# A layernorm, spectral filter and GELU block: reordered table and filter loads, and accumulating transfers released by other waits

## The chip, the cores and the metric

The kernel runs on one core of a Trainium2 chip. The time of a run is the device time in microseconds (us) of one execution. The kernel before was timed in three runs. One more execution was profiled, and every duration below comes from it.

The engines are called as in the profile: PE is TensorE (matrix multiplies, with PEld its weight loads), DVE is VectorE, ACT is ScalarE, POOL is GpSimd and SP is SyncE. SP does no arithmetic here; it issues most of the transfers, one after the other, in a fixed order.

## The reference

```python
xn = layernorm(x)                                   # x: 2048 rows of 640, bf16
A  = irfft2(rfft2(xn) * (w_r + 1j * w_i))           # filter of 2048 x 321 complex numbers
B  = gelu(xn @ w1 + b1) @ w2 + b2                   # w1: 640 x 1536, w2: 1536 x 640
out = x + A + B
```

All inputs and the output are bf16. The two Fourier transforms are two-dimensional, over the 2048 rows and the 640 columns.

## The kernel before

**Tiles.** The 2048 rows are 16 tiles of 128 (tile c holds the rows c, c+16, ...). A tile is normalized on DVE (`stats`, `mv`, and the subtraction and scaling at L709), with the power of -1/2 on POOL (L683). Normalized tiles lie in one of three buffers for two tiles each, two of which are inside `T` and one is `U`.

**The dense branch.** The normalized tile is turned into `xnT` (columns on the partitions): tiles 0 to 3 by PE (L727), tiles 4 to 15 by a transposing transfer that SP issues (L718). The first product, in blocks of 4, 2, 2, 4 and 4 tiles, reads `xnT` and the first weight matrix (both weight matrices are called `W` in the profile); a block's PE instruction has 512 columns for four tiles and 256 for two. GELU (L802, ACT) makes `gT`. The second product reads `gT` and the second matrix, whose four loads are called w2, w2#1, w2#2 and w2#3; each row of 640 outputs is a pair of PE instructions with 512 and 128 columns.

**The spectral branch.** DVE folds a normalized tile with its mirror image (L742, L746), PE multiplies it with the table `gtab` (first step along the rows, result `XV`), then with `etab` (columns; result `Xb`), then with small blocks of `mtab` (result `Y`). DVE multiplies `Y` with the filter `Wf` (L907, result `T`; eight pairs of row groups, two such products a pair: k = 0 with the real part, k = 1 with the imaginary part) and adds (L911, `Z`). The way back is `ntab` (result `U`, in three buffers, two of which lie in the old space of `gtab` and `T`), a transposing transfer of `U` into `XV` (L933, sixteen of them, v0 to v15), `getab`, and `htab`, which adds the branch to the output in PE's accumulators. For all matmuls PE's line is the helper's, L553, and for copies out of the accumulators the lines are L564 (ACT) and L565 (DVE).

**The filter's loads.** `Wf` is read by 26 transfers of SP (L548). W0 is the real part, W1 the imaginary part: #0 to #3 are direct pieces (16 runs of 10 KB), #4 to #8 are mirrored pieces in runs of 642 bytes (#4, #5, #6 of 80 KB, #7 of 10 KB, #8 of 70 KB). Wl0 and Wl1 with #0 to #3 are the mirrored pieces (80 KB each) for the second half of the pairs. A filter product waits for all nine pieces of its part:

```python
filt_ops.append(K.op([("dve", dve_us(4 * KP, 2))], pr, lambda e, _, k=k, Y=Y, TB=TB, pair=pair: e.tensor_tensor(
    ...
    reads=[Y, B_wpad] + (B_w + B_wl if pair == 7 else [B_w[k]] if pair < 3 else [B_w[k], B_wl[k]]), writes=[TB], after=ring_ops))
```

**The accumulating transfers.** x + b2 is made in 32 bit, tile by tile: ACT writes b2 into a buffer (L995), and a transfer issued by POOL adds the tile of x to it (L1013; xo0 to xo15, 128 rows of 2560 bytes written). The buffers are old space of `X` (eight tiles) and of `xnT` (eight tiles: 13, 14, 0, 4, 6, 9, 12, 15). DVE adds this to the dense branch's result (L1019, for ten tiles called kept) or to the final sum (L1028). In the kernel before, each of these sixteen transfers waits for every W0 and W1 piece to land and for the last transposes of `xnT`; those of tiles 6, 9, 12 and 15 also wait for v0 to v15.

**What sets the order.** Each engine runs its own list in order. The list comes from a planner inside the kernel, which picks among the ready steps by a rank (one number a step in the table `RANK`), with the table `LAND` of how long each transfer takes from issue to landing. SP's order is written by hand in `SPQ`:

```python
line = [key[k + "#0" if "#" not in k else k] for k in SPQ]
for a, b in zip(line, line[1:]):
    b.gate.append(a)
```

A `gate` fixes only the order, `deps` make a semaphore wait.

Of the kernel before, what the change touches and what calls it, by code (L numbers as in the profile page):

```python
# [194 lines left out]
LAG = 1.6  # L195


LAND = {"x0#0": 2.38, "x1#0": 2.35, "w1_0_0#0": 3.37, "b1t#0": 2.88, "w1_0_1#0": 3.83, "x2#0": 3.78, "w1_0_2#0": 3.84, "w1_0_3#0": 3.87, "x3#0": 4.21, "w1_0_4#0": 4.72, "w1_1_0#0": 5.66, "w1_1_2#0": 6.24, "w1_1_4#0": 6.12, "x4#0": 5.84, "g#0": 7.46, "x6#0": 7.79, "x8#0": 7.97, "x10#0": 8.16, "x12#0": 8.72, "x14#0": 3.56, "b2#0": 3.37, "W0#0": 3.66, "W0#1": 3.95, "W0#2": 5.89, "W0#3": 5.88, "W1#0": 6.17, "W1#1": 6.16, "W1#2": 6.45, "W1#3": 6.44, "e#0": 6.13, "m#0": 5.89, "n#0": 5.6, "w2#0": 3.39, "w2#1": 4.28, "w2#2": 5.16, "w2#3": 6.05, "W0#4": 6.54, "W0#5": 6.46, "W0#6": 6.38, "W0#7": 5.81, "W0#8": 5.66, "W1#4": 5.58, "W1#5": 5.5, "W1#6": 5.42, "W1#7": 4.85, "W1#8": 4.7, "i#0": 3.97, "h#0": 4.79, "xnT8#0": 3.2, "xnT9#0": 3.2, "xnT10#0": 6.58, "xnT11#0": 6.43, "xnT12#0": 6.86, "xnT13#0": 6.71, "xnT14#0": 7.14, "xnT15#0": 6.99, "v0#0": 2.9, "v1#0": 2.9, "v2#0": 2.9, "v3#0": 2.9, "v4#0": 2.9, "v5#0": 2.9, "v6#0": 2.9, "v7#0": 2.9, "v8#0": 2.9, "v9#0": 2.9, "v10#0": 2.9, "v11#0": 2.9, "v12#0": 2.9, "v13#0": 2.9, "v14#0": 2.9, "v15#0": 2.9, "xo0#0": 13.37, "out#0": 2.92, "xo1#0": 6.0, "out#1": 1.9, "xo2#0": 6.0, "out#2": 1.9, "xo3#0": 6.27, "out#3": 1.9, "xo4#0": 14.06, "out#4": 2.74, "xo5#0": 7.1, "out#5": 2.53, "xo6#0": 6.0, "out#6": 1.9, "xo7#0": 7.93, "out#7": 2.2, "xo8#0": 8.65, "out#8": 1.9, "xo9#0": 6.0, "out#9": 1.9, "xo10#0": 10.46, "out#10": 1.9, "xo11#0": 11.16, "out#11": 1.9, "xo12#0": 6.12, "out#12": 2.63, "xo13#0": 11.89, "out#13": 1.9, "xo14#0": 12.66, "out#14": 2.33, "xo15#0": 7.14, "out#15": 1.9, "out#16": 1.9, "out#17": 1.9, "xnT4#0": 4.05, "xnT5#0": 3.66, "xnT6#0": 3.2, "xnT7#0": 3.2, "Wl0#0": 4.62, "Wl0#1": 4.54, "Wl0#2": 4.46, "Wl0#3": 4.38, "Wl1#0": 4.3, "Wl1#1": 4.22, "Wl1#2": 4.14, "Wl1#3": 4.06}

LAT = {"pe": 0.2, "dve": 0.125, "act": 0.16, "pool": 0.12}  # L200

# [873 lines left out]
```

## Time and profile before

| | |
|---|---|
| runs of the kernel before | 148.05, 149.12, 149.16 us (median 149.12) |
| profiled execution, its own time | 149.41 us |
| its span, first to last instruction | 147.6 us |
| granted TensorE clock | 1.000 |
| PE busy | 142.5 us, 1734 matmuls |
| DVE busy | 116.1 us |
| ACT busy | 78.4 us |
| POOL busy | 23.7 us |
| packets of SP's queue, as a share of 16 DMA engines | 54.8% |
| packets of POOL's queue | 15.4% |

Rows of the page and of the queries name the engine, the source line and the tiles as out<-in; "x4" counts instructions, and a bracket at a row's end is the idle time before it and what ended it. Time in rows runs from the first instruction. About 1.8 us of the execution's own time lie around the span.

### The profile page before, as it was taken

The numbers are of one execution on the slowest core, as the hardware profiler recorded it, in microseconds if no ns is written. First come the engines' busy times: TensorE is split into PE (matmuls) and PEld (weight loads), VectorE is DVE, ScalarE is ACT, GpSimd is POOL, SyncE is SP. The second block draws the span as 40 slices with busy tenths as digits, with TensorE's granted clock in tenths as the row PEclk, the third lists the DMA queues.
The fourth block names the chain that finished last, engine by engine and source line by source line (L and its number), as shares of the span: only waits on it lengthen the run. The fifth ranks groups of instructions, "written<-read, shape, count | busy, mean of one in ns | idle before, by whom it ended". The sixth has DMA issues, their size and how long they took to land.

```text
span 147.6 us, 4154 instructions
## 1 busy us (share of the span) xinstructions
PE 142.5 (97%) x1734; PEld 88.5 (60%) x1734; DVE 116.1 (79%) x242; ACT 78.4 (53%) x136; POOL 23.7 (16%) x54
## 2 busy tenths in 40 slices
PE   7999999999899999999999989999999999999993
PEld 7898558988456454445464444455556666565573
DVE  2989999999895236989754977597625999899993
ACT  3113997999969876885643554870303620402300
POOL 4321112312000003995000000000002600000000
DMA  4999899699936634999999909206353891231324
GB/s 124 278 322 408 221 152 203 105 378 307 147 68 162 139 92 102 207 272 318 274 276 98 128 0 128 54 5 123 62 112 66 172 229 47 88 120 63 133 89 133
DMA packets 31810, 23.64 MB, mean 160 GB/s; under 512 B 20656, under 2 KB 28592, under 8 KB 31664
## 3 DMA queue, kind: packets, MB, share of 16 engines
q1 hardware_dynamic: 29456, 18.14, 54.8%
q0 software_dynamic: 2336, 5.25, 15.4%
q8 instruction: 13, 0.21, 0.6%
q14 instruction: 5, 0.04, 0.2%
HBM read 13.54 MB, written 2.62 MB: 110 GB/s over the span
## 4 chain that ended last, share of the span: by engine, by line
PE 67%; DMA 11%; DVE 10%; SPq 8%; issue 1%
PE ps L553 67%; SPq L548 7%; DMA X<-in_A_x_dram 6%; DMA xnT<-T 5%; DVE stats L678 4%; DVE T L907 2%; SPq L718 1%; DVE mv L681 1%; DVE T L746 1%; DVE T L742 1%; DVE Y L565 1%; DVE T L565 1%; DVE U L709 0%; DVE T L709 0%; DVE W L1028 0%
## 5 line engine op out<-in xcount | busy, mean ns | idle before, releaser
L553 PE MATMUL ps<-xnT,W 128*128 128x512 bf16 (+2 forms) x384 | 57.3, 301 | 1.0 <-DMA xnT<-T 0.9
L553 PE MATMUL ps<-W,gT 128*128 128x512 bf16 (+3 forms) x396 | 57.1, 295 | 0.0
L553 PEld LDWEIGHTS ps<-W,gT 128*128 128x128 bf16 x396 | 30.0, 98 | 23.0 <-issue 1.5
L553 PEld LDWEIGHTS ps<-xnT,W 128*128 128x128 bf16 x384 | 31.5, 98 | 19.5 <-issue 2.2
L802 ACT ACTIVATE gT<-ps,b1col 128x512 bf16<-128x512 f32 (+1 forms) x60 | 33.7, 619 | 3.8 <-PE ps L553 3.6
L1013 POOL DMA_DIRECT2D xnT<-in_A_x_dram x8 | 9.9, 2778 | 44.9 <-DMA XV<-T 44.9
L678 DVE BATCH_NORM_STATS2 stats<-X 128x6 f32<-128x320 bf16 x32 | 14.0, 476 | 2.5 <-DMA X<-in_A_x_dram 2.4
L564 ACT ACTIVATE Wf<-ps 128x960 bf16<-128x960 f32 (+1 forms) x8 | 6.7, 866 | 16.6 <-PE ps L553 16.6
L907 DVE TENSOR_TENSOR T<-Y,Wf 128x1288 bf16<-128x1288 bf16 x16 | 12.5, 824 | 0.1
L565 DVE CAST Xb<-ps 128x960 bf16<-128x960 f32 (+1 forms) x6 | 6.7, 1119 | 6.3 <-PE ps L553 6.3
L683 POOL TENSOR_TENSOR rstd<-mv,mhalf 128x2 f32<-128x2 f32 (+1 forms) x10 | 7.1, 710 | 25.0 <-DVE mv L681 25.0
L565 DVE CAST Y<-ps 128x644 bf16<-128x644 f32 x8 | 6.5, 826 | 5.4 <-PE ps L553 5.4
L564 ACT ACTIVATE Xb<-ps 128x960 bf16<-128x960 f32 (+1 forms) x6 | 6.8, 1142 | 6.4 <-PE ps L553 6.4
L1019 DVE TENSOR_TENSOR X<-ps,X 128x640 f32<-128x640 f32 x8 | 6.6, 821 | 4.4 <-PE ps L553 4.4
L746 DVE TENSOR_TENSOR T<-T 128x128 bf16<-128x128 bf16 (+1 forms) x32 | 9.0, 315 | 0.1
L1013 POOL DMA_DIRECT2D X<-in_A_x_dram x8 | 7.2, 2068 | 9.4 <-DMA Wf<-in_A_w_i_dram 9.4
L564 ACT ACTIVATE Y<-ps 128x644 bf16<-128x644 f32 x8 | 5.6, 711 | 4.4 <-PE ps L553 4.4
L911 DVE TENSOR_TENSOR Z<-T 128x644 bf16<-128x644 bf16 x16 | 7.0, 488 | 1.0 <-PE ps L553 1.0
L967 DVE TENSOR_TENSOR Wf<-Wf 128x960 bf16<-128x960 bf16 (+1 forms) x12 | 6.8, 598 | 0.6 <-ACT Wf L564 0.4
L564 ACT ACTIVATE XV<-ps 128x512 bf16<-128x512 f32 (+4 forms) x10 | 7.1, 744 | 0.4 <-PE ps L553 0.3
L553 PE MATMUL ps<-etab,XV 32*128 32x160 bf16 (+1 forms) x128 | 7.2, 232 | 0.0
L1028 DVE TENSOR_TENSOR W<-ps,xnT 128x640 bf16<-128x640 f32 (+2 forms) x10 | 6.7, 686 | 0.6 <-PE ps L553 0.6
(61 smaller groups left out, 140.6 us busy)
## 6 DMA issues: line engine op xcount, KB each, us to landing
X<-in_A_x_dram POOLq DMA_DIRECT2D x8, 320.0 KB, 10.3
xnT<-in_A_x_dram POOLq DMA_DIRECT2D x8, 320.0 KB, 10.8
out_dram<-W SPq DMA_DIRECT2D x15, 160.0 KB, 1.8
X<-in_A_x_dram SPq DMA_DIRECT2D x6, 320.0 KB, 8.5
W<-in_B_w_dram SPq DMA_DIRECT2D x4, 480.0 KB, 5.1
W<-in_B_w_dram SPq DMA_DIRECT2D x6, 192.0 KB, 4.1
W<-in_B_w_dram SPq DMA_DIRECT2D x2, 384.0 KB, 5.6
Wf<-in_A_w_r_dram SPq DMA_DIRECT2D x4, 160.5 KB, 5.6
```

What stands on the lines that cost most here:

```text
L548: return K.op([(q, 0.7 if q == "pool" else issue)], prio, lambda e, _: e.dma_start(dst, src), writes=[buf], after=after, rows=rows, gate=g ...
L553: ins = e.matmul(o_, lhsT=lw, rhs=rh, start=st, stop=sp_, skip_group_check=True)
L564: return e.activation(dst(), src(), ACT.Copy, scale=scale)
L565: return e.tensor_copy(dst(), src())
L678: o = K.op([("dve", 0.393)], pr, lambda e, _, c=c, h=h: e.bn_stats(stats[:, c, 6 * h:6 * h + 6], view(X, c * D + H2 * h, [[1, H2]])), read ...
L683: K.op([("pool", 0.65)], 500, lambda e, _, a=a, b=b: e.tensor_tensor(out=rstd[:, a:b], in0=mv[:, a:b, 1], in1=mhalf[:, a:b], op=ALU.pow), ...
L746: ring_ops.append(K.op([("dve", dve_us(4 * w, 2))], pr, lambda e, _, op=op, x1v=x1v, xfv=xfv, o_=o_, o0=o0, o1=o1, w=w: e.tensor_tensor(ou ...
L802: g_op = K.op([("act", act_us(128 * nt, 1))], pr + PRIO["gelu"] + GP[bi], lambda e, _, c0=c0, nt=nt, fc=fc, hps=hps: e.activation(gT[:, fc ...
L907: filt_ops.append(K.op([("dve", dve_us(4 * KP, 2))], pr, lambda e, _, k=k, Y=Y, TB=TB, pair=pair: e.tensor_tensor(out=view(TT, TB.slot * 8 ...
L911: K.op([("dve", dve_us(2 * KP, 2))], pr, lambda e, _, TB=TB, Z=Z, r=r, op=op: e.tensor_tensor(out=view(Zb, Z.slot * 4 * KP + r * KP, [[2 * ...
L967: K.op([("dve", dve_us(320 * n, 2))], pr + 2, lambda e, _, k=k, op=op, yo=yo, y2=y2, n=n: e.tensor_tensor(out=view(Wf, Y2 + y2.slot * 3 * ...
L1013: xo_ops[c] = K.op([("pool", 0.9)], 51 - c / 20, lambda e, _, c=c, xov=xov: e.dma_start(xov(0, D), xv[:, c, :], accum_op=ALU.add), reads=[ ...
```

## The change

The change has four edits.

1. `SPQ`: the four w2 loads move from behind the transposes of tile 9 in between the transposes of tiles 8 and 9 and behind them; the tables e (`etab`), m (`mtab`), n (`ntab`) and the piece W0#2 move from ahead of the transposes of tiles 10 and 11 to behind them, with more of the filter's pieces; the transposes v0 to v3 now stand ahead of the tables i (`getab`) and h (`htab`) in SP's list.
2. The accumulating transfers no longer wait for the filter's pieces, only for the transposes of `xnT`.
3. The accumulating transfers of tiles 0 and 4 now wait for v0 to v15 (`LATEXO`).
4. `RANK` and `LAND` are replaced throughout, so the planner orders every engine anew. The line numbers L460 to L1034 grow by one.

```diff
 RANK = """
-612 351 350 590 594 349 596 588 593 353 273 408 285 305 557 274 237 295 290 289 232 278 362 106 270 473 473 473 359 473 473 473 473 473 473 473 473 473 473 473 473 473
...
+207 636 638 328 442 633 499 402 528 524 381 384 376 364 383 345 388 389 399 471 377 380 529 659 342 542 542 542 443 542 542 542 542 542 542 542 542 542 542 542 542 542
...
-SPQ = ('x0 x1 w1_0_0 w1_0_1 x2 w1_0_2 w1_0_3 x3 w1_0_4 w1_1_0 x4 w1_1_2 w1_1_4 g x6 x8 x10 x12 xnT4 xnT5 x14 b2 W0 W0#1 xnT6 xnT7 xnT8 xnT9 w2 w2#1 w2#2 w2#3 e m n W0#2 '
-       'xnT10 xnT11 W0#3 W1 xnT12 xnT13 W1#1 W1#2 xnT14 xnT15 W1#3 W0#4 W0#5 W0#6 W0#7 W0#8 W1#4 W1#5 W1#6 W1#7 W1#8 Wl0 Wl0#1 Wl0#2 Wl0#3 Wl1 Wl1#1 Wl1#2 Wl1#3 i h').split()
+SPQ = ('x0 x1 w1_0_0 w1_0_1 x2 w1_0_2 w1_0_3 x3 w1_0_4 w1_1_0 x4 w1_1_2 w1_1_4 g x6 x8 x10 x12 xnT4 xnT5 x14 b2 W0 W0#1 xnT6 xnT7 w2 xnT8 w2#1 xnT9 w2#2 w2#3 '
+       'xnT10 xnT11 W0#2 W0#3 W1 W1#1 W1#2 e xnT12 xnT13 m n W1#3 W0#4 xnT14 xnT15 W0#5 W0#6 W0#7 W0#8 W1#4 W1#5 W1#6 W1#7 W1#8 Wl0 Wl0#1 Wl0#2 Wl0#3 Wl1 Wl1#1 Wl1#2 Wl1#3 v0 v1 v2 v3 i h v4').split()
...
+LATEXO = (0, 4)
...
         for c in range(16):
-            xo_ops[c].gate += [WL[-1], TD[15]]
-            xo_ops[c].deps += WL + list(TD.values())
+            xo_ops[c].deps += list(TD.values()) + (v_ops if c in LATEXO else [])
             xo_ops[c].deps += v_ops if c in HOME[4:] else []
```

`LAND` is one long line of numbers and is left out.

The new ranks move instructions on every engine. The first place is on DVE, where the first filter products stand. In brackets are the semaphores that a row waits for: d_46 to d_49 and d_61 to d_65 tell of the nine pieces of W0, d_50 to d_53 and d_66 to d_70 of the nine pieces of W1. Before:

```order
118 L565 CAST Xb<-ps 128x2x2x160 [waits s_pe]
119 L565 CAST Xb<-ps 128x3x2x160 [waits s_pe]
120 L565 CAST Y<-ps 128x2x322 [waits s_pe] x2
121 L907 TENSOR_TENSOR T<-Y,Wf 128x1288 [waits d_61,d_49,d_62,d_48,d_63,d_47,d_64,d_46,d_65,s_dve]
122 L907 TENSOR_TENSOR T<-Y,Wf 128x1288 [waits s_act]
123 L565 CAST Xb<-ps 128x3x2x160 [waits s_pe]
124 L907 TENSOR_TENSOR T<-Y,Wf 128x1288 [waits d_53,d_66,d_52,d_67,d_51,d_68,d_50,d_69,d_70]
125 L907 TENSOR_TENSOR T<-Y,Wf 128x1288
126 L911 TENSOR_TENSOR Z<-T 128x2x322 [waits s_dve]
```

And now (a line number is one higher than before):

```order
115 L566 CAST Xb<-ps 128x2x2x160 [waits s_pe]
116 L566 CAST Xb<-ps 128x3x2x160 [waits s_pe]
117 L566 CAST Y<-ps 128x2x322 [waits s_pe] x2
118 L908 TENSOR_TENSOR T<-Y,Wf 128x1288 [waits d_66,d_53,d_67,d_52,d_68,d_51,d_69,d_50,d_70,s_dve]
119 L908 TENSOR_TENSOR T<-Y,Wf 128x1288 [waits d_61,d_49,d_62,d_48,d_63,d_47,d_64,d_46,d_65,s_act]
120 L566 CAST Xb<-ps 128x3x2x160 [waits s_pe]
121 L1020 TENSOR_TENSOR X<-ps,X 128x640 [waits d_607]
122 L908 TENSOR_TENSOR T<-Y,Wf 128x1288 x2
123 L912 TENSOR_TENSOR Z<-T 128x2x322 [waits s_dve] x2
```

The first product to be run, once two `Xb` and two `Y` copies are done, waited for W0; it now waits for W1, whose last piece W1#8 is issued last of the eighteen. One `Xb` copy stands between the first two products and the next two in both.

The second place is on PE, from the end of the first second-product steps (pairs of 512 and 128 columns) to the first product with `etab`. Before, 8 + 7 + 10 + 8 instructions of the first product with 512 columns (`ps<-xnT,W`) stand there, and three groups with `gtab`:

```order
54 L553 MATMUL ps<-W,gT 128x512
55 L553 MATMUL ps<-W,gT 128x128
56 L553 MATMUL ps<-xnT,W 128x512 x8
57 L553 MATMUL ps<-gtab,T 128x64x2 x10
58 L553 MATMUL ps<-xnT,W 128x512 x7
59 L553 MATMUL ps<-gtab,T 128x64x2 x10
60 L553 MATMUL ps<-xnT,W 128x512 x10
61 L553 MATMUL ps<-gtab,T 128x64x2 x10
62 L553 MATMUL ps<-xnT,W 128x512 x8
63 L553 MATMUL ps<-etab,XV 128x160 x16
64 L553 MATMUL ps<-xnT,W 128x512 x5
65 L553 MATMUL ps<-etab,XV 128x160 x24
```

Now there are 2 + 8 + 7 of them at this place:

```order
54 L554 MATMUL ps<-W,gT 128x512
55 L554 MATMUL ps<-W,gT 128x128
56 L554 MATMUL ps<-xnT,W 128x512 x2
57 L554 MATMUL ps<-gtab,T 128x64x2 x10
58 L554 MATMUL ps<-xnT,W 128x512 x8
59 L554 MATMUL ps<-gtab,T 128x64x2 x10
60 L554 MATMUL ps<-xnT,W 128x512 x7
61 L554 MATMUL ps<-etab,XV 128x160 x16
62 L554 MATMUL ps<-xnT,W 128x512 x5
63 L554 MATMUL ps<-etab,XV 128x160 x24
```

Three more stand further up, between the first two blocks of second-product steps:

```order
40 L554 MATMUL ps<-W,gT 128x512
41 L554 MATMUL ps<-W,gT 128x128
42 L554 MATMUL ps<-xnT,W 128x512 x3
43 L554 MATMUL ps<-gtab,T 128x64x2 x10
44 L554 MATMUL ps<-W,gT 128x512
45 L554 MATMUL ps<-W,gT 128x128
```

So 20 instead of 33 of these 512-column instructions come ahead of the first `etab` group. One `gtab` group of ten (counted over the whole list) has moved from this stretch to a place ahead of the second product's first step; the groups ahead of `etab` are eight in both. Behind the first `etab` group both kernels run 5 instructions with 512 columns, 24 with `etab`, then 7 and 8 (now 8 and 7) with a group of `mtab` behind each.

More of the change, by code (lines that the diff above doesn't have):

```diff
@@ L195 @@
 LAG = 1.6
-LAND = {"x0#0": 2.38, "x1#0": 2.35, "w1_0_0#0": 3.37, "b1t#0": 2.88, "w1_0_1#0": 3.83, "x2#0": 3.78, "w1_0_2#0": 3.84, "w1_0_3#0": 3.87, "x3#0": 4.21, "w1_0_4#0": 4.72, "w1_1_0#0": 5.66, "w1_1_2#0": 6.24, "w1_1_4#0": 6.12, "x4#0": 5.84, "g#0": 7.46, "x6#0": 7.79, "x8#0": 7.97, "x10#0": 8.16, "x12#0": 8.72, "x14#0": 3.56, "b2#0": 3.37, "W0#0": 3.66, "W0#1": 3.95, "W0#2": 5.89, "W0#3": 5.88, "W1#0": 6.17, "W1#1": 6.16, "W1#2": 6.45, "W1#3": 6.44, "e#0": 6.13, "m#0": 5.89, "n#0": 5.6, "w2#0": 3.39, "w2#1": 4.28, "w2#2": 5.16, "w2#3": 6.05, "W0#4": 6.54, "W0#5": 6.46, "W0#6": 6.38, "W0#7": 5.81, "W0#8": 5.66, "W1#4": 5.58, "W1#5": 5.5, "W1#6": 5.42, "W1#7": 4.85, "W1#8": 4.7, "i#0": 3.97, "h#0": 4.79, "xnT8#0": 3.2, "xnT9#0": 3.2, "xnT10#0": 6.58, "xnT11#0": 6.43, "xnT12#0": 6.86, "xnT13#0": 6.71, "xnT14#0": 7.14, "xnT15#0": 6.99, "v0#0": 2.9, "v1#0": 2.9, "v2#0": 2.9, "v3#0": 2.9, "v4#0": 2.9, "v5#0": 2.9, "v6#0": 2.9, "v7#0": 2.9, "v8#0": 2.9, "v9#0": 2.9, "v10#0": 2.9, "v11#0": 2.9, "v12#0": 2.9, "v13#0": 2.9, "v14#0": 2.9, "v15#0": 2.9, "xo0#0": 13.37, "out#0": 2.92, "xo1#0": 6.0, "out#1": 1.9, "xo2#0": 6.0, "out#2": 1.9, "xo3#0": 6.27, "out#3": 1.9, "xo4#0": 14.06, "out#4": 2.74, "xo5#0": 7.1, "out#5": 2.53, "xo6#0": 6.0, "out#6": 1.9, "xo7#0": 7.93, "out#7": 2.2, "xo8#0": 8.65, "out#8": 1.9, "xo9#0": 6.0, "out#9": 1.9, "xo10#0": 10.46, "out#10": 1.9, "xo11#0": 11.16, "out#11": 1.9, "xo12#0": 6.12, "out#12": 2.63, "xo13#0": 11.89, "out#13": 1.9, "xo14#0": 12.66, "out#14": 2.33, "xo15#0": 7.14, "out#15": 1.9, "out#16": 1.9, "out#17": 1.9, "xnT4#0": 4.05, "xnT5#0": 3.66, "xnT6#0": 3.2, "xnT7#0": 3.2, "Wl0#0": 4.62, "Wl0#1": 4.54, "Wl0#2": 4.46, "Wl0#3": 4.38, "Wl1#0": 4.3, "Wl1#1": 4.22, "Wl1#2": 4.14, "Wl1#3": 4.06}
@@ new lines @@
+LAND = {"x0#0": 2.36, "x1#0": 2.39, "w1_0_0#0": 3.76, "b1t#0": 3.0, "w1_0_1#0": 3.74, "x2#0": 3.69, "w1_0_2#0": 4.21, "w1_0_3#0": 4.21, "x3#0": 4.21, "w1_0_4#0": 4.69, "w1_1_0#0": 5.25, "w1_1_2#0": 6.14, "w1_1_4#0": 7.73, "x4#0": 5.57, "g#0": 8.54, "x6#0": 8.68, "x8#0": 8.77, "x10#0": 9.05, "x12#0": 9.1, "x14#0": 4.49, "b2#0": 3.72, "W0#0": 4.5, "W0#1": 4.3, "W0#2": 6.0, "W0#3": 6.39, "W1#0": 6.78, "W1#1": 7.17, "W1#2": 7.56, "W1#3": 3.0, "e#0": 7.64, "m#0": 2.83, "n#0": 2.54, "w2#0": 3.55, "w2#1": 4.29, "w2#2": 5.02, "w2#3": 5.91, "W0#4": 3.18, "W0#5": 2.89, "W0#6": 2.89, "W0#7": 2.33, "W0#8": 2.71, "W1#4": 2.79, "W1#5": 2.8, "W1#6": 2.8, "W1#7": 2.24, "W1#8": 2.71, "i#0": 2.69, "h#0": 3.51, "xnT8#0": 4.24, "xnT9#0": 4.98, "xnT10#0": 6.6, "xnT11#0": 6.45, "xnT12#0": 4.06, "xnT13#0": 3.91, "xnT14#0": 3.69, "xnT15#0": 3.54, "v0#0": 2.9, "v1#0": 2.9, "v2#0": 2.9, "v3#0": 2.9, "v4#0": 2.9, "v5#0": 2.9, "v6#0": 2.9, "v7#0": 2.9, "v8#0": 2.9, "v9#0": 2.9, "v10#0": 2.9, "v11#0": 2.9, "v12#0": 2.9, "v13#0": 2.9, "v14#0": 2.9, "v15#0": 2.9, "xo0#0": 4.2, "out#0": 3.0, "xo1#0": 5.0, "out#1": 2.0, "xo2#0": 5.8, "out#2": 2.0, "xo3#0": 6.5, "out#3": 2.0, "xo4#0": 5.0, "out#4": 2.0, "xo5#0": 7.2, "out#5": 2.0, "xo6#0": 5.8, "out#6": 2.0, "xo7#0": 8, "out#7": 2.0, "xo8#0": 8.7, "out#8": 2.0, "xo9#0": 6.5, "out#9": 2.0, "xo10#0": 9.5, "out#10": 2.0, "xo11#0": 10.2, "out#11": 2.0, "xo12#0": 7.2, "out#12": 2.0, "xo13#0": 11, "out#13": 2.0, "xo14#0": 11.7, "out#14": 2.0, "xo15#0": 8, "out#15": 2.0, "out#16": 2.0, "out#17": 2.0, "xnT4#0": 5.07, "xnT5#0": 4.24, "xnT6#0": 4.03, "xnT7#0": 3.51, "Wl0#0": 2.79, "Wl0#1": 2.8, "Wl0#2": 2.8, "Wl0#3": 2.81, "Wl1#0": 2.81, "Wl1#1": 2.81, "Wl1#2": 2.82, "Wl1#3": 2.82}
```

34 rows, old and new, of the table RANK are left out of this document.

## The prediction

> **What bounds the kernel now.** I read the page first. Two of its rows matter:
>
> ```profile
> span 147.6 us, 4154 instructions
> PE 142.5 (97%) x1734; PEld 88.5 (60%) x1734; DVE 116.1 (79%) x242; ACT 78.4 (53%) x136; POOL 23.7 (16%) x54
> ```
>
> PE is idle for 5 of 147.6 us, so a change can win only what PE waits, and every new wait of PE counts in full. The waits of PE come next. Beside the one for the first instruction there are two:
>
> ```profile
> PE ps L553 <- DMA xnT<-T: 0.9, 1, 0.9
> PE ps L553 <- DVE T L907: 0.6, 1, 0.6
> ```
>
> PE's timeline says what they cost. Twelve second-product steps (six pairs) take 37.59 - 35.96 = 1.63 us, so the twelve from 38.15 should be followed at 39.78; PE goes on at 40.86, **1.08 us** late. Ahead of a group with small blocks the same twelve take 104.67 - 102.94 = 1.73, so the twelve from 83.67 should be followed at 85.40; PE goes on at 86.09, **0.69 us** late.
>
> ```profile
> 35.96 1.79 PE L553 MATMUL ps<-W,gT 128*128 128x512 bf16 x12
> 37.59 0.72 PE L553 MATMUL ps<-gtab,T 128*128 128x128 bf16 x10
> 38.15 1.79 PE L553 MATMUL ps<-W,gT 128*128 128x512 bf16 x12
> 40.86 1.89 PE L553 MATMUL ps<-xnT,W 128*128 128x512 bf16 x8 [0.92 <-DMA xnT<-T]
> 42.59 0.72 PE L553 MATMUL ps<-gtab,T 128*128 128x128 bf16 x10
> 49.66 0.97 PE L553 MATMUL ps<-etab,XV 128*128 128x160 bf16 x16
> ...
> 83.67 1.79 PE L553 MATMUL ps<-W,gT 128*128 128x512 bf16 x12
> 86.09 0.52 PE L553 MATMUL ps<-Z,ntab 32*32 32x320 bf16 x32 [0.62 <-DVE T L907]
> ...
> 102.94 1.80 PE L553 MATMUL ps<-W,gT 128*128 128x512 bf16 x12
> 104.67 0.51 PE L553 MATMUL ps<-Z,ntab 32*32 32x320 bf16 x32
> ```
>
> The first wait is for the transposes of tiles 10 and 11. They are issued at 31.81 and take 8.0 us, behind W2 (whose four loads take 5.1 in the median), three tables and W0#2:
>
> ```profile
> 31.81 2.73 SPq L718 DMA_TRANSPOSE xnT<-T  x2
> ...
> xnT<-T SPq DMA_TRANSPOSE x2, 8.0
> ...
> W<-in_B_w_dram SPq DMA_DIRECT2D x4, 480.0 KB, 5.1
> ```
>
> The second is named after DVE, but ACT's copy for the same group began at 85.18, after 1.60 us of waiting for a transpose of `U`, and so ended just ahead of PE's 86.09. The first two transposes of that kind took 8.8 us:
>
> ```profile
> 85.18 0.77 ACT L564 ACTIVATE U<-ps 128x512 bf16<-128x512 f32 x2 [1.60 <-DMA XV<-U]
> ...
> XV<-gtab SPq DMA_TRANSPOSE x2, 8.8
> ```
>
> These transposes share the DMA engines with the accumulating transfers, which POOL starts at 57.65, when W1's last piece has landed:
>
> ```profile
> 57.65 7.18 POOL L1013 DMA_DIRECT2D X<-in_A_x_dram  x8 [9.35 <-DMA Wf<-in_A_w_i_dram]
> ```
>
> **What the change removes.** Transposes 10 and 11 now stand behind the w2 loads alone, and those are issued some 2 us earlier. PE's first readers of them now stand right behind the first twelve second-product steps, and one group of `gtab` more (38.15 - 37.59 = 0.56) ahead of these: they are due at 37.59 + 0.56 = 38.15. The transposes are issued some 2 us earlier, near 30 and 31, and would need about 7 us to be late; the 8.0 had four more loads in it. I count this wait as gone: **-1.08**, with 0 as the other end. What is late next there is W2 for the steps now due at 35.96 + 0.56 = 36.5; its last load keeps its time, since two transposes stand among the earlier issues. For the second wait: the accumulating transfers start 10 us earlier (below), only nine of them run early, and `getab` and `htab` now stand behind v0 to v3, so the DMA engines are free for these: **-0.69**, or 0. The two tables' readers are PE's last stages, far behind. Both together are -1.77. The later place of e, m and n and of tiles 0 and 4 costs nothing as long as they land ahead of their readers, which are 3 us or more away; a table late by k us would cost k. The new order of equal work on DVE and ACT I bound by the smaller wait, -0.7 to +0.7, and take 0, since PE's queue covers it in all but two places now.
>
> **What it adds.** The filter's multiplication comes earlier. Up to the first `etab` group PE runs 13 fewer instructions of 512 columns. Eight of them take 42.59 - 40.86 = 1.73, so 13 are 2.81 us. With the wait gone, `etab` starts at 49.66 - 1.08 - 2.81 = 45.77, that is 3.89 earlier, and from there to the first filter product the work is the same. DVE's timeline has that product at 58.28:
>
> ```profile
> 38.77 1.22 DVE L565 CAST XV<-ps 128x1024 bf16<-128x1024 f32 x1
> 40.86 0.80 DVE L709 TENSOR_SCALAR T<-X,mv,rstd 128x640 bf16<-128x640 bf16 x2 [0.87 <-DMA xnT<-T]
> ...
> 58.28 1.57 DVE L907 TENSOR_TENSOR T<-Y,Wf 128x1288 bf16<-128x1288 bf16 x2
> 59.77 1.23 DVE L565 CAST Xb<-ps 128x960 bf16<-128x960 f32 x1
> 60.89 1.56 DVE L907 TENSOR_TENSOR T<-Y,Wf 128x1288 bf16<-128x1288 bf16 x2
> 65.41 1.57 DVE L907 TENSOR_TENSOR T<-Y,Wf 128x1288 bf16<-128x1288 bf16 x2
> ```
>
> So DVE is ready for it at 58.28 - 3.89 = **54.4**. Before, the first product read the real part W0; W1 was wanted only at 60.89. Now the first one reads W1, the last to land.
>
> When is W1#8 issued? SP first waits for the norm of tile 12. DVE starts it at 40.86, after 0.87 of waiting for the old transposes. That wait goes, and the reordered work ahead of it nets to some 1.9 us less (an estimate: two `XV` copies of 1.22 and shorter work go behind it, about half as much comes ahead). So it starts near 38.1 and ends, as one of two in 0.80, near 38.55. From there SP goes by its rows:
>
> ```profile
> 30.18 0.44 SPq L548 DMA_DIRECT2D mtab<-c_M  x1
> 41.33 2.54 SPq L718 DMA_TRANSPOSE xnT<-T  x2
> 45.18 2.60 SPq L718 DMA_TRANSPOSE xnT<-T  x2
> 48.46 3.86 SPq L548 DMA_DIRECT2D Wf<-in_A_w_r_dram  x5
> 52.36 3.16 SPq L548 DMA_DIRECT2D Wf<-in_A_w_i_dram  x5
> ...
> xnT<-T SPq DMA_TRANSPOSE x2, 2.9
> ```
>
> Two transposes take 2.58 (to the next issue), m and n twice 0.48, W1#3 and W0#4 twice 0.65: transpose 14 is issued at 43.4, 15 at 44.7, and it lands 2.9 later, at 47.6 to 47.7. **At 47.7 the accumulating transfers are let go.** SP goes on at 46.1: the five pieces W0#4 to #8 took 52.36 - 48.46 = 3.9, so #5 to #8 take 3.25; then W1#4 from 49.4, at 0.64 each, W1#8 at 52.0. So W0#8 (48.7) and all of W1#4 to #8 are issued after the accumulations began. The trace shows what that does to such loads, as KB and us to landing:
>
> ```profile
> Wf<-in_A_w_i_dram SPq DMA_DIRECT2D x3, 80.2 KB, 2.6
> Wf<-in_A_w_i_dram SPq DMA_DIRECT2D x1, 70.2 KB, 2.4
> ...
> Wf<-in_A_w_i_dram SPq DMA_DIRECT2D x1, 80.2 KB, 6.0
> ...
> Wf<-in_A_w_i_dram SPq DMA_DIRECT2D x1, 80.2 KB, 8.4
> ...
> X<-in_A_x_dram POOLq DMA_DIRECT2D x1, 320.0 KB, 6.1
> ...
> xnT<-in_A_x_dram POOLq DMA_DIRECT2D x4, 320.0 KB, 17.0
> ```
>
> Ahead of the accumulations an 80 KB piece lands after 2.6 us and W1#8 after 2.4. The four that SP issues right behind POOL's start at 57.65 take 6.0 (issued at 58.14, landed at 64.1) up to 8.4 (60.11, 68.5): the first lands 6.5 us after POOL's start, the others 1.46 apart. The accumulations land 6.1 after the first issue and, by the last row (17.0 from 62.9, nine to ten behind the first), about 1.7 apart.
>
> The contested pieces are now 70 + 3 x 80 + 10 + 70 = 390 KB, or 4.87 of 80 KB. By the trace's pattern W1#8 lands at 47.7 + 6.5 + 3.87 x 1.46 = 59.8. Without the slow first one, from W0#7's landing (47.4 + 2.6 = 50.0), it is 50.0 + 4.87 x 1.46 = 57.1. With no contention it is 52.0 + 2.4 = 54.4, just in time. I take the middle of the first two, **58.5**, since they rest on the nearest rows: the same loads beside the same transfers. DVE then waits 4.1 us (bounds 0 and 5.4). Behind the product on DVE stands the `Xb` copy for the third row group, which PE awaits for its third `mtab` group:
>
> ```profile
> 61.25 0.49 PE L553 MATMUL ps<-Xb,mtab 32*32 32x322 bf16 x32
> ```
>
> The copy ended at 59.77 + 1.23 = 61.00, 0.25 ahead of PE; PE has one more instruction of 0.22 ahead of that group now. So PE is covered for some 0.5, and waits **+3.6** (0 to +4.9).
>
> The same happens once more: the fourth pair reads Wl1, eight pieces on. Its product comes 65.41 - 58.28 + 0.78 = 7.9 after the first, at 66.4. Nine accumulations end near 47.7 + 6.1 + 8 x 1.7 = 67.4; by then some six of the eight have landed at 1.46 apart, and the rest follow at 0.64: 68.5. Of these 2.1 us I take **+0.8** (0 to +2.1) for PE, under half, as PE's queue between two groups covers part.
>
> [...]
>
> **The sum.** 149.41 - 1.77 + 3.6 + 0.8 = 152.0 against the profiled execution. That one lies 0.3 above the median of 149.12, so I say **151.7**.
>
> **The rivals.** *The loads escape* (faster). If the accumulations get going late, or yield, W1#8 lands before 54.9 (54.4 plus the cover), and only the removed waits count: 149.12 - 1.77 = 147.35. For it: POOL's first accumulation was slow, 6.1 us; undisturbed, W1#8 is in time. Against it: four such loads in the same company took 6.0 to 8.4. If POOL is still held by something else, say by ACT's copies of b2, the change doesn't do what it says, and the time is the same 147.35.
> *Mild contention* (no change). W1#8 lands at 55 to 57.7, PE waits 0.1 to 2.8, and Wl1 is no longer late: 147.45 to 150.1, say 149.
> The forecast, on the slower side, decides from there: at 58 PE's wait of 3.1 less 1.77 is near 1%.
>
> [...]
>
> **How the numbers follow.** A comparison of this kernel tells about 1% from no change, 147.6 to 150.6. Forecast: 0.62, with a range of its own from 150.3 (W1#8 near 58, nothing for Wl1) to 153.8 (59.8 and Wl1 late by 2.1). Mild: 0.22. Escape: 0.16. These are the three chances of slower, same and faster. The range reaches from 147.5, which leaves out most of the escape, to 153.8.
>
> **What would show it.** Right: PE's wait at 39.8 is gone; ACT's wait for `U`'s transposes is gone, and v0 to v3 land within 4 us; POOL starts near 48; W1#4 to #8 land after 5 to 8 us; DVE waits 2 to 5 us for a load of `Wf` near 54, and PE for `Xb` right behind. Wrong: W1#8 landing within 3 us of its issue, or a DVE wait that PE doesn't repeat.

## The result, and the profile after

The changed kernel takes 156.53 us in the median of four executions (155.11 to 157.62) against 149.14 for the kernel before (148.05 to 149.19): a ratio of 1.048, with a 95% interval of 1.038 to 1.058. The forecast was 151.7 and its range ended at 153.8. Executions more than 1.5% above the fastest of the same kernel are left out of all ratios, here the one of 157.62. The direction was right, and five microseconds were missing.

The profiled execution took 155.11 us, 5.70 more than that of before. Its page has a row that the page of before lacks: PEclk, printed when the granted TensorE clock leaves 1.0.

```profile
span 153.3 us, 4135 instructions
PE 143.0 (93%) x1717; PEld 87.9 (57%) x1734; DVE 114.4 (75%) x239; ACT 80.0 (52%) x139; POOL 23.4 (15%) x54
...
PEclk9999999999999999689999999999999999999999
```

PE now idles for 10.3 us where it idled for 5.1 (17 of its 1734 records are missing after the change and count as idle). The list of PE's waits names the longest (total, times, longest):

```profile
PE ps L554 <- DVE Xb L566: 3.0, 1, 3.0
```

DVE's timeline shows where it comes from (start, length, and in the bracket the idle time ahead): DVE waits 3.46 us for the last piece of W1, does two products and then the `Xb` copy that PE wants.

```profile
59.79 1.57 DVE L908 TENSOR_TENSOR T<-Y,Wf 128x1288 bf16<-128x1288 bf16 x2 [3.46 <-DMA Wf<-in_A_w_i_dram]
61.28 1.24 DVE L566 CAST Xb<-ps 128x960 bf16<-128x960 f32 x1
```

PE's timeline has the same wait, and more:

```profile
57.72 1.90 PE L554 MATMUL ps<-xnT,W 128*128 128x512 bf16 x8
62.57 0.77 PE L554 MATMUL ps<-Xb,mtab 32*32 32x322 bf16 x32 [2.95 <-DVE Xb L566]
63.67 3.51 PE L554 MATMUL ps<-W,gT 128*128 128x128 bf16 x17 [0.33 <-issue]
67.11 0.49 PE L554 MATMUL ps<-Xb,mtab 32*32 32x322 bf16 x32
```

The last three rows are the second loss. The 32 small matmuls take 0.77 at 62.57 and 0.49 at 67.11, and the second-product steps between them are as slow. Busy times by the microsecond, with the granted clock as the third number from the end, show why: the clock is at half speed from 62.5 to 66.

```profile
61.00:62.00 1.00, 0.00 (x0) 0.00 (x0) 1.00 (x2) 0.00 (x0) 0.00 (x0) 1.00 1.11 266
62.00:63.00 1.00, 0.43 (x32) 0.21 (x32) 1.00 (x2) 0.00 (x0) 0.00 (x0) 0.77 1.13 269
63.00:64.00 1.00, 0.67 (x34) 0.39 (x4) 1.00 (x3) 0.01 (x1) 0.00 (x0) 0.50 1.14 264
...
65.00:66.00 1.00, 1.00 (x6) 0.45 (x4) 1.00 (x4) 0.44 (x1) 0.00 (x0) 0.53 1.12 178
66.00:67.00 1.00, 1.00 (x10) 0.49 (x7) 0.32 (x1) 0.00 (x0) 0.00 (x0) 1.00 0.40 59
```

Over the whole execution the clock's mean is 0.989; in the other three it is 0.976, 0.978 and 0.978. As 1.1% of 153.3 us is 1.7 us, the profiled execution lost one stretch of 3.4 us at half clock (62.53 to 65.95, at 0.50). By the same sum the others, with spans of 153.9 to 155.8 us, lost 3.4 to 3.7 us, as much as two such stretches: an estimate, as they have no profile.

The third loss is a wait that should have gone. The timeline of PE's weight loads shows it best: twelve second-product steps begin at 37.30 and take 1.63, so the next should start at 38.93. It starts at 40.06, **1.13** later, when the transpose of tile 11 has landed (40.00).

```profile
37.30 1.56 PEld L554 LDWEIGHTS ps<-W,gT 128*128 128x128 bf16 x12
40.06 0.34 PEld L554 LDWEIGHTS ps<-xnT,W 128*128 128x128 bf16 x3 [1.20 <-issue]
```

The list of transfers issued between 30 and 35 (KB each, median us to landing) has these transposes still at 7.0 us, with two pieces of W2 just ahead of them:

```profile
W<-in_B_w_dram SPq DMA_DIRECT2D x2, 480.0 KB, 5.9
...
xnT<-T SPq DMA_TRANSPOSE x2, 7.0
```

(The releaser is called "issue" there: a wait for a transfer does not always get its name.) Two smaller losses remain. In the first 36 us PE is busy for 33.98 (before 34.84), and in the 12 us from 108 for 11.42 (before 12.00). Together: 2.95 for the wait, 1.56 for the clock (below), 0.86 early, 0.6 late, less 0.7 for the wait at 86 that is gone. That is 5.3 of the 5.7 us, against this one profile of before; a second one, below, shows that not all of it belongs to the change.

### The profile page after: what moved, and what is told of

Read it like the earlier page. It is cut to its first block, busy times and chain, and to the rows that moved or that the text cites. A ratio compares the mean times of both kernels' runs of the same rounds, so it can differ in the third digit from the quotient of the medians.

```text
span 153.3 us, 4135 instructions
## 1 busy us (share of the span) xinstructions
PE 143.0 (93%) x1717; PEld 87.9 (57%) x1734; DVE 114.4 (75%) x239; ACT 80.0 (52%) x139; POOL 23.4 (15%) x54
## 4 chain that ended last, share of the span: by engine, by line
PE 50%; DVE 23%; DMA 11%; SPq 11%; issue 4%; DVEq 0%
PE ps L554 50%; SPq L549 7%; DVE stats L679 6%; DMA Wf<-in_A_w_i_dram 5%; DMA X<-in_A_x_dram 4%; DVE T L747 4%; DVE T L743 3%; SPq L719 3%; DVE T L710 2%; DMA XV<-gtab 2%; DVE X L1020 1%; DVE mv L682 1%; DVE XV L566 1%; DVE U L710 1%; DVE Xb L566 1%
## 5 line engine op out<-in xcount | busy, mean ns | idle before, releaser
L554 PE MATMUL ps<-xnT,W 128*128 128x512 bf16 (+2 forms) x384 | 58.1, 300 | 1.4 <-issue 0.9
L554 PE MATMUL ps<-W,gT 128*128 128x128 bf16 (+3 forms) x381 | 56.3, 296 | 1.5 <-issue 1.0
L554 PEld LDWEIGHTS ps<-W,gT 128*128 128x128 bf16 x396 | 30.8, 99 | 24.2 <-issue 2.4
L554 PEld LDWEIGHTS ps<-xnT,W 128*128 128x128 bf16 x384 | 30.9, 98 | 20.1 <-issue 3.9
L565 ACT ACTIVATE Wf<-ps 128x960 bf16<-128x960 f32 (+1 forms) x6 | 5.3, 879 | 24.0 <-PE ps L554 24.0
L566 DVE CAST Y<-ps 128x644 bf16<-128x644 f32 x7 | 5.8, 827 | 7.3 <-PE ps L554 7.3
L565 ACT ACTIVATE Y<-ps 128x644 bf16<-128x644 f32 x9 | 6.4, 707 | 7.9 <-PE ps L554 4.2
L1020 DVE TENSOR_TENSOR X<-ps,X 128x640 f32<-128x640 f32 x8 | 6.6, 821 | 3.2 <-PE ps L554 3.2
L565 ACT ACTIVATE XV<-ps 128x512 bf16<-128x512 f32 (+4 forms) x11 | 8.2, 782 | 0.8 <-PE ps L554 0.8
L566 DVE CAST Wf<-ps 128x960 bf16<-128x960 f32 (+1 forms) x6 | 6.2, 1040 | 1.9 <-PE ps L554 1.9
L1029 DVE TENSOR_TENSOR W<-ps,X 128x640 bf16<-128x640 f32 x8 | 6.5, 818 | 0.7 <-PE ps L554 0.7
```

Source lines behind the costliest of these rows:

```text
L554: ins = e.matmul(o_, lhsT=lw, rhs=rh, start=st, stop=sp_, skip_group_check=True)
L565: return e.activation(dst(), src(), ACT.Copy, scale=scale)
L566: return e.tensor_copy(dst(), src())
L1020: kept_ops.append(K.op([("dve", dve_us(D))], 30, lambda e, _, kps=kps, xov=xov: e.tensor_tensor(out=xov(0, D), in0=psb(kps.slot, [[1, D]]) ...
```

## The experiments

The edits stand right behind `K.schedule()`, where the orders of all engines are fixed. So they change a wait, a place in one queue or the work in one step, and no other order. All ratios are against the kernel before on the same chip. Each run has a label, given ahead of its edit: a_ stands for the changed kernel, b_ for the kernel before.

### What holds the filter's loads up

a_wait: let the accumulations wait for the loads again.

```diff
+for o in xo_ops.values():
+    o.deps = o.deps + WL
```

> The changed kernel in its own order, but the accumulating transfers wait again for the filter's loads. Theory (the accumulations hold the loads up, and TensorE's long wait then halves its clock for 3.4 us): W1#8 lands some 2.7 us after its issue, near 54.8, DVE does not wait for it, TensorE's wait of 2.95 at 59.6 and the stretch at half clock (worth 1.7) are gone, clock 1.000, time 155.1 - 2.95 - 1.7 = 150.4, or up to 151.1 if the first transposes of U are late again as they were before. Rival (the loads are late for a reason of their own, such as how SP issues them in the new order): W1#8 still lands after 57 and the time stays at 155 to 157.

155.77 us, ratio 1.044 (1.035 to 1.052); the profiled execution took 157.85. Both theories were wrong about the time. The loads do escape: the last piece of W1 lands 2.5 us after its issue, and DVE no longer waits for it. But in the new order the addition of tile 2's accumulated rows (L1020) stands right behind the `Xb` copy, and now it is that transfer which is late. PE waits for the accumulator that this addition frees. The list of transfers, DVE's timeline and PE's:

```profile
Wf<-in_A_w_i_dram SPq DMA_DIRECT2D x1, 70.2 KB, 2.5
```

```profile
63.55 0.83 DVE L1020 TENSOR_TENSOR X<-ps,X 128x640 f32<-128x640 f32 x1 [4.72 <-DMA X<-in_A_x_dram]
```

```profile
64.83 4.58 PE L554 MATMUL ps<-W,gT 128*128 128x128 bf16 x17 [5.06 <-DVE X L1020]
```

The new order is built on early accumulations; taking them away costs about as much as it gives.

b_free, the other way round: release the accumulations in the kernel before.

```diff
+for o in xo_ops.values():
+    o.deps = [d for d in o.deps if d not in WL]
```

> The kernel before with one part of the change alone: its accumulating transfers no longer wait for the filter's loads; every order is as before. Theory (contention): they start near 49.3, W0#6 to W1#8 land 5 to 8 us after their issue, W1#8 near 62.4, when DVE has wanted it since 60.9; but in this order the Xb copy stands ahead of that product, so TensorE waits at most about 1 us, its clock stays at 1.000, and the transposes of U lose their 0.7 us: 148.5 to 149.8. Rival (the loads are not slowed by the accumulations): they land 2 to 3 us after their issue, and only the 0.7 is won, 148.4.

156.71 us, ratio 1.053 (1.047 to 1.060), with the clock at 0.978 or 0.989. This one edit, in the old order, costs as much as the whole change. The loads are even later than in the changed kernel, since twelve accumulations run beside them and SP itself is held: it issues W1#8 at 58.06 where it did at 54.93, and the piece takes 9.1 us. Contention is shown from both sides; my estimate of 1 us for PE was far too low, since W1#8 was put at 62.4 and landed at 67.1: SP was held, and the pieces took 6 to 9 us. The list of transfers issued from 50 to 60:

```profile
Wf<-in_A_w_i_dram SPq DMA_DIRECT2D x3, 80.2 KB, 7.9
...
Wf<-in_A_w_i_dram SPq DMA_DIRECT2D x1, 70.2 KB, 9.1
```

And PE's timeline:

```profile
69.52 0.77 PE L553 MATMUL ps<-Xb,mtab 32*32 32x322 bf16 x32 [5.33 <-ACT Y L564]
```

a_two: so keep early only the two accumulations that the new order wants first.

```diff
+for c, o in xo_ops.items():
+    if c not in (1, 2):
+        o.deps = o.deps + WL
```

> The changed kernel in its own order, with only two accumulating transfers early: those of tiles 1 and 2 start as they do now, and the other seven wait for the filter's loads. (Tile 2's is the one that the order wants first, behind the Xb copy.) Theory (the load W1#8 is late because each piece has to share the DMA engines with the accumulations, so fewer of them mean less delay): W1#8 lands at 55 to 56.5 where it landed at 59.7, TensorE's wait of 2.95 and its stretch at half clock are gone, clock 1.000; the last pieces for the second pair of row groups may now cost 0.5. Time 155.1 - 2.95 - 1.65 = 150.5, up to 151. Rival (one accumulation in flight is enough to hold all of the loads): W1#8 still lands after 58.5 and the time is 154 to 156.

150.86 us, ratio 1.016 (1.007 to 1.024), clock 1.000 (0.999 once). As expected: W1#8 takes 4.6 us, PE's long wait is gone, and so is the stretch at half clock. Moving the start of seven transfers gives back 5.7 of the 7.4 us. This run also gives the price of the slow clock. From one `mtab` group to the next PE takes 62.67 - 59.69 = 2.98 here, and took 67.11 - 62.57 = 4.54 with the same instructions in the changed kernel: **1.56**. PE's timeline of this run:

```profile
59.69 0.49 PE L554 MATMUL ps<-Xb,mtab 32*32 32x322 bf16 x32
60.34 2.39 PE L554 MATMUL ps<-W,gT 128*128 128x128 bf16 x17 [0.16 <-issue]
62.67 0.49 PE L554 MATMUL ps<-Xb,mtab 32*32 32x322 bf16 x32
```

### What a wait of PE costs beside itself

a_fill: ten useless matmuls in the wait of the changed kernel, ahead of the last 512-column sums before it (they write where these sums then start anew):

```diff
+o = next(o for o in K.order["pe"] if o.name == "hps4_9")
+...
+    for _ in range(10):
+        e.matmul(psb(slot, [[1, 512]]), lhsT=view(W1, 128 * 9, [[1, 128]]), rhs=xnT[:, 12:16, 0, :], start=True, stop=True, skip_group_check=True)
```

> The changed kernel with ten useless matmuls of 512 columns (10 x 0.216 = 2.2 us) put into the stretch in which TensorE waits for the Xb copy; their sums are overwritten. Theory (the clock falls because TensorE is idle): the wait left is 0.8 us, the clock stays at 1.000, and the kernel gets faster by the 1.7 us of one stretch at half clock against its own profiled 155.1, so 153.4, though TensorE does more. Rival (the clock falls for another cause, such as the crowd of transfers): clock 0.98 as now and 155 to 157.

154.22 us, ratio 1.036 (1.029 to 1.043), clock 0.995 to 1.000 in all four executions. More work, and 1.9 us less by the ratios (1.048 and 1.036): the clock fell because PE was idle, not because of the transfers, which are the same. (In the profiled execution, with 0.998, the windows from 50 to 120, the wait among them, have 1.00, and the one from 120 to 152 has 0.98.) PE's timeline has the useless matmuls and the 0.45 that is left of the wait:

```profile
57.94 2.32 PE L1049 MATMUL ps<-xnT,W 128*128 128x512 bf16 x10
...
61.79 0.50 PE L554 MATMUL ps<-Xb,mtab 32*32 32x322 bf16 x32 [0.45 <-DVE Xb L566]
```

b_hold4, b_hold8 and b_hold16: now the wait alone, in the kernel before, by useless statistics on DVE ahead of its first filter product; n is 4, 8 or 16.

```diff
+o = next(o for o in K.order["dve"] if o.name == "T0")
+...
+    for c in range(n):
+        e.bn_stats(stats[:, c, 0:6], view(Yb, y, [[1, H2]]))
```

> The kernel before with eight useless statistics of 320 elements (8 x 0.40 = 3.2 us) on DVE ahead of its first filter product; their results go to cells no longer read. No transfer is moved. Theory (a wait of TensorE of about 3 us costs more than itself): TensorE waits some 2.9 us for the Xb copy near 61, and then runs at half clock for 3.4 us or 6.8 us: 149.1 + 2.9 + 1.7 = 153.7, or 155.4. Rival (the wait costs what it lasts): clock 1.000 and 152.0.

> The kernel before with four useless statistics (4 x 0.40 = 1.6 us) on DVE ahead of its first filter product, half of the earlier dose. [...]

> The kernel before with sixteen useless statistics (16 x 0.40 = 6.4 us) on DVE ahead of its first filter product. [...]

| n | PE's wait in the profile | ratio (interval) | executions, us (granted clock) |
|---|---|---|---|
| 4 | 1.3 | 1.010 (1.006 to 1.013) | 149.80, 149.91, 150.08, 150.25 (all 1.000) |
| 8 | 2.9 | 1.028 (1.020 to 1.036) | 151.87, 152.81 (1.000), 153.41 (0.989), 154.06 (0.976) |
| 16 | 6.0 | 1.059 (1.053 to 1.065) | 156.68, 156.78, 157.12, 158.68 (all 0.978) |

The waits stand in the lists of PE's waits, in the order of the table:

```profile
PE ps L553 <- DVE Xb L565: 1.3, 1, 1.3
PE ps L553 <- DVE Xb L565: 2.9, 1, 2.9
PE ps L553 <- DVE Xb L565: 6.0, 1, 6.0
```

A wait of 1.3 us costs itself. With 6.0 the clock was 0.978 in all four executions; 2.2% of the profiled one's 156.6 us is 3.4 us, what two stretches of 3.4 us at half clock lose. In b_hold8 it fell in two executions of four. Only the profiled execution's wait is known, so how long it was in the other three is open. No transfer was moved here, so the wait is cause enough.

The traces say more. In the changed kernel the clock falls to 0.50 at 62.53, behind a wait of 2.95 us that ends at 62.57, and is back at 1.00 at 65.95. In b_hold8's profile, behind a wait of 2.87, the mean clock is 1.000. The three longest waits (5.06 in a_wait, 5.33 in b_free, 6.0 in b_hold16) come with a mean clock of 0.978 each, over spans of 155.9, 155.6 and 156.6 us; from these I estimate some 6.8 us at half. So in these five profiles one wait of some 2.9 us brought the half clock and one did not, and the three over 5 us all did. What decides it at some 2.9 us is not shown.

### The waits that were to go

b_v: getab and htab behind v0 to v3, and tiles 0 and 4 late, in the kernel before (`behind` moves entries of SP's list):

```diff
+behind(["i#0", "h#0"], "v3#0")
+for c in (0, 4):
+    xo_ops[c].deps = xo_ops[c].deps + v_ops
```

> The kernel before with another part of the change alone: getab and htab stand behind the first four transposes of U (v0 to v3) in SP's queue, and the accumulations of tiles 0 and 4 wait for the last transpose of U. Nothing else moves. Theory (v0 to v3 are slow because of these transfers): they land within 5 us of their issue where the first took 9.6, ACT does not wait for them at 85, and TensorE's 0.69 there is gone: 148.8 - 0.7 = 148.1. Rival (ten accumulations are enough to keep v0 to v3 late): no difference, 148.8.

149.10 us, ratio 1.002 (0.999 to 1.006): no gain. In the trace the wait for `U`'s transposes is gone. The next run, b_again, is the kernel before, unchanged, in a second profile, and says why nothing is won by that.

> The kernel before once more, for a second profile. The profile of before has x4 landing at 10.95 and the transposes of tiles 4 and 5 at 20.53 and 21.05; the kernels since, which are the same until 40 in four cases, have these at 11.08 to 11.67 and at 21.35 to 21.93, and TensorE 0.3 to 0.9 us behind from there on. If that is chance, this profile lies among them, 0.3 to 0.5 behind the first one at 24; if the first profile is typical, it has TensorE's first product of tiles 4 and 5 at 21.1.

148.56 us. ACT waits 0.71 for these transposes where it waited 1.60, and PE does not wait for its copy at all. The three b_hold profiles, where these transfers are as before, have no such wait of PE either. The 0.69 of the first profile was that execution's, not the kernel's. ACT's timeline:

```profile
84.25 0.77 ACT L564 ACTIVATE U<-ps 128x512 bf16<-128x512 f32 x2 [0.71 <-DMA XV<-U]
```

It also weighs the two smaller losses, 0.86 in the first 36 us and 0.6 from 108 on, in the same windows (PE's busy time is the first number behind the comma):

```profile
0.00:36.00 36.00, 34.45 (x375) 28.44 (x376) 31.77 (x102) 23.59 (x50) 9.23 (x36) 1.00 0.89 249
108.00:120.00 12.00, 11.79 (x127) 7.68 (x127) 8.76 (x14) 4.22 (x6) 3.58 (x4) 1.00 0.71 160
```

In the first window it is 34.45; five more profiles with the old first stage have 33.79 to 34.86, and six with the new one 33.79 to 34.62. What I expected, 0.3 to 0.5 behind the first profile, is what it is (0.39). Both ranges are nearly the same, so most of that 0.86 is chance. From 108 on the second profile has 11.79 where the first had 12.00, so 0.2 of that 0.6 is not the change's.

b_vw: then W2's pieces earlier, and the small loads out of the transposes' way, on top of b_v:

```diff
+behind(["W0#0", "W0#1", "e#0", "m#0", "n#0", "W0#2"], "xnT11#0")
+behind(["w2#0"], "b2#0")
+behind(["w2#1"], "xnT7#0")
```

> The kernel of the last experiment, and in SP's queue the first piece of W2 moved to the place where the first two pieces of W0 stood, its second piece behind the transpose of tile 7, and two tables of the filter's stage, a third and three pieces of W0 behind the transposes of tiles 10 and 11. Theory (these transposes are late because 1.9 MB of W2 and 0.5 MB of others stand ahead of them and drain at some 380 GB/s until 38; two pieces sent earlier, into a gap of the DMA engines, bring them forward): tiles 10 and 11 land before 37 where they landed at 40.1 and 40.8, TensorE's wait of 1.08 near 39.8 is gone: 148.8 - 0.7 - 1.1 = 147.0. Rival (a transpose takes its 7 to 8 us there whatever stands ahead, or W2 so early delays the transposes of tiles 6 and 7): 148.1 or slower.

148.45 us, ratio 0.998 (0.995 to 1.002). The transposes land at 35.2 and 35.9, and PE's wait of a microsecond is gone. So it was what stood ahead of them. This run moves W2's pieces and the small loads together; in the changed kernel the tables and W0#2 are out of the way too, but W2's last piece lands at 36.6 (34.5 here), and the transposes at 37.9 and 40.0. The time did not follow: the interval holds no change, and no run shows where the microsecond went.

### The last stage

a_late: tile 11's accumulation behind the last transpose of `U`, in the changed kernel:

```diff
+xo_ops[11].deps = xo_ops[11].deps + v_ops
```

> The changed kernel, with one transfer moved: the accumulation of tile 11, which now runs beside the last transposes of U (v11 to v15), waits for them. Theory (that accumulation makes v11 to v15 take 2.7 to 4.8 us, v15 is a microsecond late, and DVE's and ACT's copies behind it cost TensorE 0.75 between 109 and 119): v11 to v15 land 2.6 to 2.8 us after their issue, and TensorE's loss there falls to 0.3 or less. Rival (the order of DVE behind v15 costs it): v15 lands earlier, and TensorE still loses 0.6 to 0.8 there. The rest of the kernel is as it was, with its long wait and the clock that falls by chance, so the total is not the measure here.

154.85 us in one execution. v11 and v12 are fast now (2.7, 2.6), but v13 still takes 4.3 and v15 is nearly as late; PE is busy for 11.36 of the 12 us from 108, as in the changed kernel (11.42). That accumulation is not the cause. The busy time in a window counts missing records as idle, so here is another measure: from the twelve second-product steps at 115.00 to the `htab` group at 119.44 in the changed kernel PE takes 4.44, and from the same to the same here 4.50. In this execution PE's wait was in two parts, 1.83 and 1.30, and the clock stayed at 1.000.

What falls on v13 in both traces is a read of 16 KB on the queue for code (109.5 in the changed kernel, 108.8 here). In a_fill40, forty matmuls of 128 columns in place of a_fill's ten of 512 move it:

```diff
-    for _ in range(10):
-        e.matmul(psb(slot, [[1, 512]]), ..., rhs=xnT[:, 12:16, 0, :], ...)
+    for _ in range(40):
+        e.matmul(psb(slot, [[1, 128]]), ..., rhs=xnT[:, 12, 0, :], ...)
```

> The changed kernel with forty useless matmuls of 128 columns (40 x 0.056 = 2.2 us) in the stretch in which TensorE waits for the Xb copy, where the earlier filled kernel had ten of 512: the same time, but thirty more instructions (and their weight loads), so that TensorE's next fetches of code (16 KB on a queue of their own, one for some 128 matmuls) come some 2 us earlier against the work. Theory (a fetch that falls beside a transpose stretches it from 2.6 to 4.4 us, and the change's order lets one fall on v13, which makes v15 late by 0.8 and costs TensorE 0.75 between 109 and 119): the fetch now falls on v11 or before, v12 to v15 take 2.6 to 2.9 each, and the loss there is 0.3 or less. Rival (the order of DVE and ACT behind v15 costs it): the loss stays at 0.6 to 0.8 wherever the fetch falls. The clock stays near 1.000 as in the earlier filled kernel.

153.03 us in one execution. The read now falls beside v11, v12 and v13, which take 6.4, 4.6 and 4.0. v15 is in time, though, and PE is busy in all of the 12 us from 108 (the window's row, PE's time the first behind the comma):

```profile
108.00:120.00 12.00, 12.00 (x113) 7.33 (x112) 9.10 (x14) 3.91 (x5) 5.38 (x6) 1.00 0.77 169
```

Between the groups named above PE takes 3.72, 0.72 less. That speaks for the place of the read, as an order that was at fault would lose the same. It rests on one execution, the transposes were not as fast as I had said, and in a_fill, where the read falls beside v11 to v13 as well, the same stretch takes 4.12. I take it as likely in part, not shown.

### The gains without the costs

b_best: the kernel before with b_v's edit and, in SP's list:

```diff
+behind(["W0#0", "W0#1", "e#0", "m#0", "n#0", "W0#2"], "xnT11#0")
+behind(["w2#0", "w2#1"], "xnT7#0")
```

> The kernel before with the two gains of the change and none of its costs: getab and htab behind v0 to v3 and the accumulations of tiles 0 and 4 behind the last transpose of U, as in the two experiments before; W2's first two pieces behind the transpose of tile 7 (so nothing more stands ahead of tiles 4 to 7 than in the kernel before, and 320 KB of W0 less), and three pieces of W0 and the tables e, m and n behind the transposes of tiles 10 and 11. The accumulations still wait for the filter's loads. Theory: tiles 10 and 11 land before 38, both waits of TensorE are gone, 149.1 - 1.0 - 0.7 = 147.4, or 147.8 if the last stage gives 0.4 back as it did in those experiments. Rival (the early stage or the last one gives all back): 148.5 to 149.

148.07 us against 148.71, ratio 0.996 (0.994 to 0.999): the one version that beats both kernels, by 0.4%. One of its twelve executions, left out of the ratio, took 154.42 with a clock of 0.978, which no trace here explains; the clock of the kernel before was 0.999 or more in all 47 executions beside these experiments. With that one the means differ by 0.1%, so a gain on average is not shown. The wait near 39.8 is gone: PE's timeline has no bracket where it had 0.92.

```profile
39.29 1.79 PE L553 MATMUL ps<-W,gT 128*128 128x512 bf16 x12
40.92 1.89 PE L553 MATMUL ps<-xnT,W 128*128 128x512 bf16 x8
```

The forecast of 147.4 counted 0.7 for a wait that an ordinary execution does not have.

## Why the prediction was wrong

**The mechanism was right.** POOL's timeline and the list of transfers issued from 46 on, both of the changed kernel:

```profile
48.58 6.29 POOL L1014 DMA_DIRECT2D X<-in_A_x_dram  x7 [2.02 <-DMA xnT<-U]
```

```profile
Wf<-in_A_w_i_dram SPq DMA_DIRECT2D x3, 80.2 KB, 6.2
...
Wf<-in_A_w_i_dram SPq DMA_DIRECT2D x1, 70.2 KB, 7.7
```

POOL starts at 48.58 (forecast near 48). W1#4 to #8 take 5.5 to 7.7 us (5 to 8), and W1#8 lands at 59.7, the upper end of 57.1 to 59.8. DVE waits 3.46 (2 to 5), PE 2.95 right behind it (3.6). That these waits came out so near is partly luck: W1#8 landed 1.2 later than the 58.5 of the sum, but DVE was ready 1.9 later too, at 56.33 and not 54.4. a_two, b_free and the loads of a_wait show that the accumulations do it. Behind W1#4 the pieces landed 1.36 to 1.66 apart (the 10 KB one 0.34), near the 1.46 of the forecast; its lower figure of 57.1 did not follow, since the first piece beside the accumulations, W0#8, landed 2.9 us after the last one ahead of them (53.14 and 50.20) and W1#4 another 1.8 later. SP's issue of W1#8 was on time (52.05, forecast 52.0). The escape by POOL being held did not occur.

**The step that failed most is one that is not in the sum: a wait of PE was priced at its length.** The prediction let every new wait of PE count "in full", and no more. But the wait of 2.95 us halved the clock for 3.4 us afterwards. That stretch cost 1.56 in the profiled execution. The other three executions have mean clocks of 0.976 to 0.978, worth two stretches by the estimate above, some 3 of the 4.8 us by which the median missed the forecast. a_fill and the b_hold runs show that the wait does it.

**The wait for tiles 10 and 11: -1.08 forecast, about 0 measured.** "Would need about 7 us to be late" was the condition, and 7.0 is what they took. I had counted the loads ahead and not their bytes. W2's 1.9 MB stood ahead of them as before, and its last piece was issued at 30.29, later than the 29.01 of before. The transposes were issued at 30.98 and 32.87, not near 30 and 31. b_vw and b_best show what it takes: W2's first pieces earlier, with the small loads out of the way.

**The wait at 86: -0.69 forecast and measured** (v0 to v3 took 2.7 to 4.5 us where they took 5.7 to 9.6), but b_again shows that an ordinary execution of the kernel before does not have it.

**The second wait for Wl1: +0.8 forecast, 0 measured.** DVE was forecast to want Wl1 at 66.4 and wanted it at 69.2: 1.3 of that is the first product, at 59.79 and not 58.5, and 1.5 the slow clock, for which DVE waited on PE. All of Wl1 had landed by then (67.9, forecast 68.5). A late engine meets later transfers in time.

**Not foreseen:** about 0.6 in the last stage, 0.2 of it within what two profiles of one kernel differ by, and up to 0.9 in the first, most of it chance.

**The range was added up wrongly as well.** Its upper end was to be W1#8 at 59.8 and Wl1 late by 2.1: 149.12 - 1.77 + 4.9 + 2.1 = 154.35, not 153.8. The measured 156.5 lies above both.

## What to carry over

Price a new wait of PE by what comes after it, too: here a wait of 1.3 us cost its length, one of 2.9 to 3.0 brought 3.4 us at half clock or none, and each one over 5 brought, by the mean clocks of 0.978, an estimated 6.8. Before a wait is counted as removable, look for it in a second profile of the same kernel, and count the bytes ahead of the transfer that it waits for, not the instructions. A transfer that is let go early is neither good nor bad: ask which of them the order needs first, and release those.

## What the hardware showed that I had not expected

- TensorE's granted clock fell to one half (0.50) behind a wait of 2.95 us for 3.4 us, and behind waits of 5.06, 5.33 and 6.0, by the mean clocks of 0.978, for an estimated 6.8. Behind one of 2.87 it stayed at 1.000. With 2.2 us of useless matmuls inside the wait the mean clock was 0.995 to 1.000.
- SP is slowed as well, though not at once: the first six loads issued after POOL's start at 48.58 came 0.64 apart, and from 52.05 on SP issued them 1.3 to 1.9 us apart. Its timeline has four in 6.47 us, where five took 3.86 before:

```profile
53.37 6.47 SPq L549 DMA_DIRECT2D Wf<-in_A_w_r_dram  x4
```

- A transpose that takes 2.6 us took 3.9 to 4.4 when a 16 KB read on the code queue (0.9 to 1.7 us in the profiles of before and after) fell on it: v6 and v7 in the kernel before (4.4 and 3.9), v7 and v13 in the changed one (4.4 each). In these two profiles the slow transposes of the later stage that stood beside no accumulation all had such a read beside them. The reverse does not hold: v8 and v12 in the kernel before were issued during such a read and took 2.6 and 2.7.
